# Recurrence, dense layer and expert layer in one program: chunks two to six issued as the source has them, attention units moved and stretched, expert rows fetched one slot earlier, scattered writes without mutual order

## The chip, the cores and the metric

One core of one Trainium2 chip runs the whole program in one launch. The metric is device time in microseconds (us), from the host-independent measurement of one execution; for the kernel before it is the median of three runs.

## What is computed

Three layers follow one another on 4 sequences of 768 tokens, 3072 tokens in all, 320 features.

```
for t in range(S):                       # gated recurrence, 8 heads of 40, per sequence
    m_new = max(f[t] + m, i[t])
    C = exp(f[t]+m-m_new) * C + exp(i[t]-m_new) * outer(v[t], k[t])
    n = exp(f[t]+m-m_new) * n + exp(i[t]-m_new) * k[t]
    y[t] = sigmoid(o[t]) * (C @ q[t]) / max(|n . q[t]|, 1)
x = y as 3072 x 320
h = x @ w_in;  x = (h * sigmoid(h)) @ w_out            # 320 -> 2048 -> 320
logits = x @ w_gate;  e = argmax(logits);  p = softmax(logits)[e]
out[token] = p * (relu(x @ w1[e]) @ w2[e])             # one of 8 experts, 320 -> 1024 -> 320
```

## The kernel before

**Tiles and stages.** A sequence is cut into 6 chunks of 128 tokens. A *unit* is one chunk of one sequence of the recurrence, all 8 heads, in closed form; there are 24, and the first four are done in a prologue. A unit's steps have names in the code: `load_unit` and `load_lam` (DMA in; `lam` is a 128x1024 table of gate sums, broadcast over partitions from `lam_d`, L202), `mask_lam` (POOL, L207), `prep_qk` (splits q and k in two halves of 16 bits; two DMA transposes, L230 and L234), `prep_exp` (ScalarE, L241), `at_S` (scores, matmuls L294, multiplied by `lam` on VectorE, L296), `at_I` and `at_C` (read and update of the state; its new halves are copied by two DMAs, L378 and L379), `at_PV` (matmuls L318, then a VectorE run that ends in y: L324 to L341), `at_X` (y is transposed on TensorE, L394, and read out by L397 on ScalarE and L400 on VectorE). The scores, state, PV and X results of all units share two PSUM buffers (`ps_at`, L66).

**The dense layer** takes chunk by chunk, 512 tokens of all four sequences at once, in 16 steps. A step is eight 128x512 matmuls (L959), a tanh on ScalarE (L975), a product on VectorE (L978), a 16-bit copy on ScalarE (L983) and its rest on VectorE (L986), and, two steps later (`LAG = 2`), twelve 128x328 matmuls (L1003 to L1005). Units of chunk c+1 are done beside the dense layer of chunk c. After a chunk, `rows(c)` picks the expert of each token, finds its place in a table `rows_x` in HBM and scatters the token there (indirect DMA of POOL, L929).

**The order.** Each step has two *slots* p. A table `plan` says at which slot a piece is traced; what a piece leaves to do is traced a slot later. The first slots of the units are in `base`; weights of experts 0 to 3 are loaded (`load_w`, L540 to L542, three DMAs of 704 KB together) and converted at slots of their own (L837). The traced order is only the source's: up to the end of chunk six the Tile scheduler sorts the instructions of each engine by its own cost model. From there, inside `tc.manual_schedule` (L1290), TensorE, ScalarE, VectorE and SyncE keep the order of the source. SyncE issues nearly all DMAs, one after another.

**The expert layer** is a line of 28 *places* of 128 rows each (three early ones, then three per expert, then four whose expert is a value read at run time). `get` (L1280) reads a row number from SBUF into a SyncE register (L1180), fetches 128 rows by a DMA transpose (L1183) into one of four buffers (Qs and Ks) and two numbers per row (L1188). `m_half` is 32 matmuls (L1203), twice per place; `m_l2` is 24 matmuls (L1222 to L1224) of the place before, a VectorE multiply (L1226), and an indirect DMA that scatters 128 finished rows into the output (L1234). Between them the weights of experts 4 to 7 and of the last four places are loaded into six staging buffers, three of them (`more`) free only from place 5 on, and converted on ScalarE and VectorE. To the scheduler all scatters write one tensor, the output.

```
        base = {n: PU * (n - B) - 2 for n in range(B, NC * B)}
        ...
            at(p + 4, at_PV, *cb)
            at(p + 4 + 3, at_X, *cb)
```

Of the kernel before, what the change touches and what calls it, by code (L numbers as in the profile page):

```python
# [8 lines left out]
F32 = mybir.dt.float32  # L9
# [24 lines left out]
def mlstm_moe_kernel(ctx, tc, q, k, v, ig, fg, og, w_in, w_out, w_gate, w1, w2, out):  # L34
    nc = tc.nc
# [13 lines left out]
    NG = 4  # L49
# [101 lines left out]
    vw_b, hb_b = carve(FIRST, (H, D1)), carve(FIRST, (H, D1))  # L151
    y_b = carve(FIRST, (384,))
    cl_b = carve(FIRST, (H, D1), F16)[0:D]
# [160 lines left out]
    def at_PV(c, b):  # L314
# [5 lines left out]
        def tail():  # L320
# [13 lines left out]
            nc.vector.reciprocal(out=den, in_=den)  # L334
            yt = y_b
            y = yt[:, 0:DM].rearrange("p (h d) -> p h d", d=D)
# [234 lines left out]
    with contextlib.nullcontext():  # L571
# [217 lines left out]
        def at(p, fn, *args):  # L789
            plan.setdefault(p, []).append((fn, args))  # L790


        PU = 2 * NF // B
        base = {n: PU * (n - B) - 2 for n in range(B, NC * B)}
        for i in range(B):
            base[B + i] = (1, 8, 15, 19)[i]
        for n in range(B, NC * B):
# [4 lines left out]
            if n > B:  # L802
                at(max(p - 9, base[n - 1] - 3), load_lam, *cb)
            at(p - 7, prep_qk, *cb)
# [7 lines left out]
            if cb[0] < NC - 1:  # L812
                at(p + 3, at_C, *cb)
            at(p + 4, at_PV, *cb)
            at(p + 4 + 3, at_X, *cb)

# [19 lines left out]
        for i in range(4 * NG):  # L836
            p = 2 * NF * 2 + 10 * i if i < 2 * NG else 2 * NF * (NC - 1) + 3 + 7 * (i - 2 * NG) // 2  # L837
            at(p, lambda i=i: w_go.append(load_w(i // NG, i % NG, i // NG)))
            at(p + (8 if i < 2 * NG else 7), lambda: w_go.pop(0)())
# [4 lines left out]
        def rows(c, b0=0, b1=B):  # L844
# [92 lines left out]

            return [experts, place, scale, weights] + [lambda b=b: halves(b) for b in range(nb)]

# [117 lines left out]
        passes = [(c, 0, B) for c in range(NC)]  # L1057
        p = 0
        for c, b0, b1 in passes:
            for f in range(NF):  # L1060
                tanh, prod, high, low = l1(c, f, b0, b1)
# [25 lines left out]
        while plan or late:  # L1087
            p = min([*plan, *late])
            run_late(p)
            run_at(p)  # L1090
        mp = ctx.enter_context(tc.tile_pool(name="mp", bufs=3, reuse_waits="tile"))
        rt = ctx.enter_context(tc.tile_pool(name="rt", bufs=1, reuse_waits="tile"))
# [119 lines left out]

        turn = [0]

        def m_l2(i, k, no):
# [16 lines left out]
            else:  # L1232
                nc.vector.tensor_tensor(out=sid, in0=no, in1=xm.pop(i)[:, 1:2], op=ALU.add)  # L1233
            nc.gpsimd.indirect_dma_start(  # L1234
                out=out[:, :], out_offset=bass.IndirectOffsetOnAxis(ap=sid, axis=0),
                in_=y, in_offset=None, bounds_check=NT - 1, oob_is_err=False,
            )


# [40 lines left out]
        def get(i):  # L1280
            if NE <= i < len(line):
                fetch(line[i][0], line[i][2])
# [4 lines left out]
        for _ in range(3):  # L1287
            load(None)
        ENG = mybir.EngineType
        with tc.manual_schedule(engines={ENG.PE, ENG.Activation, ENG.DVE, ENG.SP}):  # L1290

            for cf in todo:
                l2(*cf)
            for i in range(2):
                rowt.append(th_v[i][:, 0:RW])
                nc.gpsimd.memset(rowt[-1][:, 352:384], 0.0)
            experts, place, scale, weights, *halves = rows(NC - 1)
            half = lambda i, r: m_half(line[i][0], line[i][1], r)
# [19 lines left out]
            second(0)  # L1318
            for i in range(NE, NE + 2):
                get(i)  # L1320
            for i in range(2, len(line)):
                if i > 2:
                    get(i + 2)
                t = half(i, 0)
# [10 lines left out]
                split()  # L1335
                if i == 5:
                    for x in more:
                        load(x)
                second(i - 1)
# [42 lines left out]
```

## Time and profile before

| | us |
|---|---|
| median of 3 runs (lowest, highest) | 773.44 (769.42, 777.27) |
| the profiled execution, device time | 771.19 |
| its span, first to last instruction | 769.5 |
| TensorE busy in the span | 674.0 (88%) |
| VectorE, ScalarE busy | 516.6, 374.5 |
| mean granted TensorE clock | 0.947 |

Times in the profile count from the first instruction. Chunk one of the dense layer begins at 46.9, chunks two to six at 159.6, 247.2, 326.4, 406 and 478.7; the expert places begin at 538.1, and TensorE's last matmul ends at 757.0. The granted clock is a share of 2.4 GHz; it has two levels, 1.0 and 0.5. "DMA share" is the time that packets took, as a share of the core's 16 DMA engines.

### The profile page before, as it was taken

To read this page: it belongs to the slowest core of one execution; us is meant where nothing else is said; L and a number is where in the kernel's file an instruction comes from. 1 tells how busy PE (TensorE), PEld (TensorE's weight loads), DVE (VectorE), ACT (ScalarE), POOL (GpSimd) and SP (SyncE) were. 2 spreads that over 40 slices of the span, in tenths; PEclk is the share of its full clock that TensorE was granted. 3 is DMA by queue.
4 is the path that set the end of the run, shared out by engine and by line. 5 is a ranking of instruction groups with operands and counts; after the bars stand their busy time and mean duration, and the time that the engine had idled before them with its cause. 6 is when DMAs were issued, how large, how long until landed. Compare 5 with 4: busy or idle time off the path is not lost.

```text
span 769.5 us, 15581 instructions
## 1 busy us (share of the span) xinstructions
PE 674.0 (88%) x5840; PEld 477.4 (62%) x5840; DVE 516.6 (67%) x1262; ACT 374.5 (49%) x816; POOL 102.5 (13%) x134
## 2 busy tenths in 40 slices
PE   4858999998787898988999898999898799988993
PEld 3725766765444465655665564556787677777882
DVE  6777788895888776667577775844686275656631
ACT  4654466676656455555477434543334244334420
POOL 3110101102101121002100200110211021111211
PEclk9867799999999999998999999999999799999997
DMA  8767999987889855454533315420258999999800
GB/s 157 147 140 205 212 169 213 233 167 167 181 176 180 140 126 101 93 93 93 114 77 73 97 39 149 125 63 2 61 128 183 153 195 187 178 181 166 152 15 14
DMA packets 242827, 102.81 MB, mean 134 GB/s; under 512 B 181141, under 2 KB 236632, under 8 KB 242744
## 3 DMA queue, kind: packets, MB, share of 16 engines
q1 hardware_dynamic: 239380, 92.98, 61.7%
q0 software_dynamic: 2880, 8.68, 3.3%
q8 instruction: 48, 0.79, 0.5%
q14 instruction: 35, 0.29, 0.1%
q10 hardware_dynamic: 484, 0.08, 0.1%
HBM read 71.64 MB, written 11.59 MB: 108 GB/s over the span
## 4 chain that ended last, share of the span: by engine, by line
PE 42%; DMA 22%; DVE 15%; ACT 8%; issue 6%; SPq 3%; POOL 2%; POOLq 0%; ACTq 0%; DVEq 0%
PE ps_h L959 11%; PE ps_m L1203 9%; DMA w_all<-lam_d 5%; DMA Qs<-rows_x 4%; DMA out_dram<-ym,sid 3%; PE ps_y L1000 3%; DMA e<-in_moe_w_dram 3%; PE ps_pv L318 3%; ACT w_all L241 2%; DMA w_all<-Qs 2%; PE ps_y L1003 2%; DVE w_all L978 2%; PE ps_y L1004 2%; PE ps_y L1005 2%; POOL w_all L207 2%
## 5 line engine op out<-in xcount | busy, mean ns | idle before, releaser
L959 PE MATMUL ps_h<-w_all 128*128 128x512 f16 x768 | 197.1, 398 | 5.5 <-ACT w_all L466 3.5
L959 PEld LDWEIGHTS <-w_all 128*128 128x128 f16 x768 | 75.2, 102 | 84.0 <-issue 15.2
L1203 PEld LDWEIGHTS <-w_all 128*128 128x128 f16 x1792 | 105.8, 100 | 25.2 <-DMA Qs<-rows_x 13.0
L1003 PE MATMUL ps_y<-w_all 128*128 128x328 f16 x332 | 101.0, 304 | 2.0 <-ACT w_all L1011 2.0
L1004 PE MATMUL ps_y<-w_all 128*128 128x328 f16 x332 | 100.7, 303 | 0.0
L1005 PE MATMUL ps_y<-w_all 128*128 128x328 f16 x332 | 100.6, 303 | 0.0
L1208 ACT ACTIVATE hh<-ps_m 128x512 f16<-128x512 f32 x56 | 33.3, 595 | 132.6 <-PE ps_m L1203 120.0
L986 DVE SCALAR_TENSOR_TENSOR w_all<-w_all 128x512 f16<-128x512 f32 x83 | 57.2, 689 | 48.5 <-ACT w_all L983 48.0
L983 ACT ACTIVATE w_all<-w_all 128x512 f16<-128x512 f32 x83 | 51.8, 624 | 49.2 <-DVE w_all L978 48.6
L1209 DVE SCALAR_TENSOR_TENSOR hl<-ps_m,hh 128x512 f16<-128x512 f32 x56 | 38.5, 689 | 54.1 <-ACT hh L1208 53.4
L978 DVE SCALAR_TENSOR_TENSOR w_all<-w_all,ps_h 128x512 f32<-128x512 f32 x83 | 56.6, 682 | 24.9 <-ACT w_all L975 24.6
L241 ACT ACTIVATE w_all<-w_all,bias_t 128x128 f32<-128x128 f32 x160 | 52.9, 392 | 40.2 <-POOL w_all L207 40.1
L1224 PE MATMUL ps_m<-w_all,hl 128*128 128x320 f16 x224 | 67.0, 299 | 0.0
L1222 PE MATMUL ps_m<-w_all,hh 128*128 128x320 f16 x224 | 67.0, 299 | 0.0
L1223 PE MATMUL ps_m<-w_all,hh 128*128 128x320 f16 x224 | 67.0, 299 | 0.0
L1203 PE MATMUL ps_m<-Qs,w_all 128*128 128x128 f16 x896 | 54.8, 224 | 13.5 <-DMA Qs<-rows_x 11.7
L975 ACT ACTIVATE w_all<-ps_h 128x512 f32<-128x512 f32 x83 | 48.6, 586 | 34.3 <-PE ps_h L959 33.3
L1203 PE MATMUL ps_m<-Ks,w_all 128*128 128x128 f16 x896 | 54.1, 222 | 7.4 <-DMA Ks<-rows_x 6.7
L207 POOL TENSOR_SCALAR_AFFINE_SELECT w_all<-w_all 128x1024 f32<-128x1024 f32 x20 | 24.4, 1219 | 233.7 <-DMA w_all<-lam_d 146.2
L1234 POOL DMA_INDIRECT out_dram<-ym,sid x28 | 32.0, 1141 | 176.3 <-DVE sid L1233 128.5
L318 PEld LDWEIGHTS ps_pv<-w_all 128*128 128x128 f32 x384 | 50.2, 205 | 6.5 <-issue 2.1
L318 PE MATMUL ps_pv<-w_all 128*128 128x41 f32 x384 | 49.9, 291 | 3.1 <-issue 1.5
(213 smaller groups left out, 1152.6 us busy)
## 6 DMA issues: line engine op xcount, KB each, us to landing
e<-in_moe_w_dram SPq DMA_DIRECT2D x34, 320.0 KB
w_all<-lam_d SPq DMA_DIRECT2D x20, 512.0 KB
e<-in_moe_w_dram SPq DMA_DIRECT2D x34, 256.0 KB
w_all<-in_moe_w_out_dram SPq DMA_DIRECT2D x16, 320.0 KB
w_all<-in_moe_w_dram SPq DMA_DIRECT2D x14, 320.0 KB
e<-in_moe_w_dram SPq DMA_DIRECT2D x34, 128.0 KB
wi<-in_moe_w_in_dram SPq DMA_DIRECT2D x8, 512.0 KB
w_all<-in_k_dram SPq DMA_DIRECT2D x24, 160.0 KB
```

The source lines that it names most:

```text
L241: nc.scalar.activation(out=lt[:, h, :], in_=lt[:, h, :], func=AF.Exp, bias=bias_t[:, c, b * H + h:b * H + h + 1])
L318: nc.tensor.matmul(pv[:, h, :], u["lam"][:, h, :], u["v"][:, h, :], start=True, stop=True)
L959: nc.tensor.matmul(ps, a, x, start=(i == 0), stop=(i == len(terms) - 1))
L978: nc.vector.scalar_tensor_tensor(out=th, in0=th, scalar=1.0, in1=ps, op0=ALU.add, op1=ALU.mult)
L986: nc.vector.scalar_tensor_tensor(out=gl, in0=th, scalar=SG, in1=gh, op0=ALU.mult, op1=ALU.subtract)
L1003: nc.tensor.matmul(ps, gh[:, ts], woh[:, f, :], start=(f == 0), stop=False)
L1004: nc.tensor.matmul(ps, gh[:, ts], wol[:, f, :], start=False, stop=False)
L1005: nc.tensor.matmul(ps, gl[:, ts], woh[:, f, :], start=False, stop=(f == NF - 1))
L1203: nc.tensor.matmul(ps[:, jj, :], w1c[k][:, a, f * 128:f * 128 + 128], x[:, m, :], start=(n == 0), stop=(n == len(terms) - 1),)
L1222: nc.tensor.matmul(ps, hh[:, f, :], w[:, 0, :], start=(f == 0), stop=False)
L1223: nc.tensor.matmul(ps, hh[:, f, :], w[:, 1, :], start=False, stop=False)
L1224: nc.tensor.matmul(ps, hl[:, f, :], w[:, 0, :], start=False, stop=(f == NF2 - 1))
```

## The change

Four things change, and what is computed stays the same.

1. `tc.manual_schedule` is entered at chunk two (`c == 1`) and left after the last planned piece, so that TensorE, ScalarE, VectorE and SyncE keep the source's order there too. POOL stays with the scheduler, as does chunk one.
2. The units' slots. From chunk four's on, a unit begins 7 slots earlier relative to the dense steps (`- 9` instead of `- 2`); chunk three's four begin at 27, 34, 41, 48 (were 30, 38, 46, 54). `at_PV` comes a slot later, `at_X` eight or twelve slots after the unit's first (was seven), `load_lam` no earlier than six slots after the start of the unit two before. y gets a second buffer. Loads of experts 2 and 3 begin 10 slots earlier. `rows` does its `place` after `scale` and `weights`.
3. Places are fetched three ahead instead of two, and the three staging buffers `more` are taken one at places 5, 6 and 7 each, not all at 5.
4. The scatters into the output are declared independent of each other.

```diff
-    y_b = carve(FIRST, (384,))
+    y_b = turns([carve(FIRST, (384,)), const.tile([128, 384], F32, name="y2")])
...
-        base = {n: PU * (n - B) - 2 for n in range(B, NC * B)}
-        for i in range(B):
-            base[B + i] = (1, 8, 15, 19)[i]
+        base = {n: PU * (n - B) - 9 for n in range(B, NC * B)}
+        for i, p in enumerate((1, 8, 15, 19, 27, 34, 41, 48)):
+            base[B + i] = p
...
-                at(max(p - 9, base[n - 1] - 3), load_lam, *cb)
+                at(max(p - 9, base[n - 1] - 3, base[n - 2] + 6 if n > B + 1 else 0), load_lam, *cb)
...
-            at(p + 4, at_PV, *cb)
-            at(p + 4 + 3, at_X, *cb)
+            at(p + 5, at_PV, *cb)
+            at(p + (8 if n < 2 * B else 12), at_X, *cb)
...
-            p = 2 * NF * 2 + 10 * i if i < 2 * NG else 2 * NF * (NC - 1) + 3 + 7 * (i - 2 * NG) // 2
+            p = 2 * NF * 2 + 10 * i if i < 2 * NG else 2 * NF * (NC - 1) - 7 + 7 * (i - 2 * NG) // 2
...
-            return [experts, place, scale, weights] + [lambda b=b: halves(b) for b in range(nb)]
+            return [experts, scale, weights, place] + [lambda b=b: halves(b) for b in range(nb)]
...
+        by_hand = {ENG.PE, ENG.Activation, ENG.DVE, ENG.SP}
+        in_order = ExitStack()
         for c, b0, b1 in passes:
+            if c == 1:
+                in_order.enter_context(tc.manual_schedule(engines=by_hand))
...
+        in_order.close()
...
+            for other in outs:
+                tc.declare_no_dep(put.ins, other.ins, reason="every token is written by one slot")
+            outs.append(put)
...
-            for i in range(NE, NE + 2):
-                get(i)
+            get(NE)
+            get(NE + 1)
             for i in range(2, len(line)):
-                if i > 2:
-                    get(i + 2)
+                get(i + 3)
...
-                if i == 5:
-                    for x in more:
-                        load(x)
+                if more and i > 4:
+                    load(more.pop(0))
```

How the instructions stand on SyncE for one unit of the middle chunks, before: the last lines are the unit's `lam` (L202), its v, its o and the next unit's k and q; L378 and L379 copy the new state of the unit that runs now.

```order
L234 DMA_TRANSPOSE w_all<-Qs_108 128x8x128
L378 DMA w_all<-w_all 40x328
L230 DMA_TRANSPOSE w_all<-Ks_110 128x8x128
L379 DMA w_all<-w_all 40x328
L202 DMA w_all<-lam_d 128x8x128
L182 DMA w_all<-in_v_dram 128x8x40
L189 DMA w_all<-in_o_gate_dram 128x8x40
L176 DMA w_all<-in_k_dram 128x8x40
L177 DMA w_all<-in_q_dram 128x8x40
```

And with the change, the same engine and stage:

```order
L378 DMA w_all<-w_all 40x328
L379 DMA w_all<-w_all 40x328
L202 DMA w_all<-lam_d 128x8x128
L230 DMA_TRANSPOSE w_all<-Ks_110 128x8x128
L234 DMA_TRANSPOSE w_all<-Qs_108 128x8x128
L176 DMA w_all<-in_k_dram 128x8x40
L177 DMA w_all<-in_q_dram 128x8x40
L182 DMA w_all<-in_v_dram 128x8x40
L189 DMA w_all<-in_o_gate_dram 128x8x40
```

Both times `lam` stands behind a pair of state copies. By the slots (copies at a unit's +5, `lam` at the unit's -9, units 8 apart) the pair now belongs to the unit two before, whose state is done two slots earlier; before, the scheduler had put `lam` behind the copies of the unit just before it.

On SyncE in the expert layer, before, around place 5: two of the staged loads (L540 to L542, into w_all) and then the fetch of place 8 into buffer Qs_107.

```order
L540 DMA w_all<-in_moe_w_dram 128x2x256
L541 DMA w_all<-in_moe_w_dram 128x1x256
L542 DMA w_all<-in_moe_w_dram 128x2x320
L540 DMA w_all<-in_moe_w_dram 128x2x256
L541 DMA w_all<-in_moe_w_dram 128x1x256
L542 DMA w_all<-in_moe_w_dram 128x2x320
L1180 TENSOR_LOAD kofi
L1180 ISA x2
L1183 ISA
L1183 DMA_TRANSPOSE Qs_107<-rows_x 128x6x128
L1188 ISA
L1188 DMA xms<-rows_x 128x2
```

And with the change (lines of the expert layer are numbered six higher there):

```order
L1186 TENSOR_LOAD kofi
L1186 ISA x2
L1189 ISA
L1189 DMA_TRANSPOSE Qs_107<-rows_x 128x6x128
L1194 ISA
L1194 DMA xms<-rows_x 128x2
L540 DMA e_6516<-in_moe_w_dram 128x2x256
L541 DMA e_6516<-in_moe_w_dram 128x1x256
L542 DMA e_6516<-in_moe_w_dram 128x2x320
L540 DMA w_all<-in_moe_w_dram 128x2x256
L541 DMA w_all<-in_moe_w_dram 128x1x256
L542 DMA w_all<-in_moe_w_dram 128x2x320
```

Twelve load DMAs stood between the fetches of places 7 and 8; now three do (those of place 4), and the loads that were staged ahead of it follow it, one at a time.

## Rows read from the trace of the kernel before

**Rows 1.** The page, part 4: shares of the chain that ended last.
```profile
PE 42%; DMA 22%; DVE 15%; ACT 8%; issue 6%; SPq 3%; POOL 2%; POOLq 0%; ACTq 0%; DVEq 0%
```
**Rows 2.** Busy time by stretch: us, then PE, PEld, DVE, ACT, POOL, clock, DMA.
```profile
46.90:159.60 112.70, 104.92 (x633) 71.60 (x633) 91.62 (x201) 67.11 (x190) 12.36 (x12) 0.90 0.89 196
159.60:247.20 87.60, 73.70 (x561) 45.50 (x558) 68.72 (x171) 52.07 (x110) 13.07 (x13) 0.96 0.90 176
159.60:478.70 319.10, 284.72 (x2131) 179.11 (x2129) 228.52 (x588) 176.48 (x384) 41.25 (x40) 0.97 0.59 121
478.70:538.10 59.40, 58.05 (x347) 33.63 (x347) 35.71 (x90) 26.65 (x49) 4.17 (x6) 1.00 0.24 66
538.10:757.00 218.90, 197.56 (x2469) 169.34 (x2467) 126.09 (x280) 78.49 (x127) 35.09 (x31) 0.97 0.76 141
601.40:712.60 111.20, 100.66 (x1233) 86.37 (x1233) 65.50 (x119) 44.44 (x70) 15.27 (x14) 0.96 1.02 180
```
**Rows 3.** Waits of TensorE, 159.6 to 478.7: who on whom, total us, times, longest.
```profile
PE ps_x L394 <- DVE w_all L340: 11.0, 5, 2.4
PE ps_s L294 <- DVE w_all L400: 9.6, 8, 2.8
PE ps_r L877 <- DVE cum L870: 3.3, 2, 1.7
```
**Rows 4.** The chain that ended last, 300 to 319 us: start, us, what.
```profile
300.51 4.07 DMA w_all<-lam_d
...
304.73 1.10 POOL w_all L207
...
307.44 1.46 ACT w_all L241 x5
...
318.65 3.99 DMA w_all<-lam_d
```
**Rows 5.** DMA issues in chunk two, 159.6 to 247.2.
```profile
e<-in_moe_w_dram SPq DMA_DIRECT2D x10, 320.0 KB
```
**Rows 6.** Waits of ScalarE, 159.6 to 478.7.
```profile
ACT w_all L241 <- POOL w_all L207: 38.4, 14, 5.4
...
ACT w_all L552 <- DMA e<-in_moe_w_dram: 17.2, 7, 4.5
```
**Rows 7.** Waits of TensorE in the expert layer, 538.1 to 757.
```profile
PE ps_m L1203 <- DMA Qs<-rows_x: 11.7, 4, 7.9
PE ps_m L1203 <- DMA Ks<-rows_x: 6.7, 3, 3.1
```
**Rows 8.** The chain that ended last, matmuls of single places.
```profile
601.45 6.06 PE ps_m L1203 x64
610.77 3.57 PE ps_m L1203 x64
617.61 3.57 PE ps_m L1203 x64
...
656.96 6.43 DMA Qs<-rows_x
...
680.40 5.39 PE ps_m L1203 x64
```
**Rows 9.** SyncE's issues in order of time, 640 to 657 us.
```profile
641.17 2.01 SPq L1183 DMA_TRANSPOSE Ks<-rows_x  x1
...
647.87 1.27 SPq L1183 DMA_TRANSPOSE Ks<-rows_x  x1
...
656.96 1.84 SPq L1183 DMA_TRANSPOSE Qs<-rows_x  x1
```
**Rows 10.** VectorE in order of time, the last row numbers (sid).
```profile
754.27 0.15 DVE L1233 TENSOR_TENSOR sid<-neg,xms 128x1 int32<-128x1 f32 x1
...
757.53 0.15 DVE L1233 TENSOR_TENSOR sid<-neg,xms 128x1 int32<-128x1 f32 x1
```
**Rows 11.** POOL in order of time, the last two scatters.
```profile
754.70 0.98 POOL L1234 DMA_INDIRECT out_dram<-ym,sid  x1 [5.86 <-DVE sid L1233]
759.70 0.98 POOL L1234 DMA_INDIRECT out_dram<-ym,sid  x1 [4.03 <-DMA out_dram<-ym,sid]
```

More of the change, by code (lines that the diff above doesn't have):

```diff
@@ L334, in tail @@
             nc.vector.reciprocal(out=den, in_=den)
-            yt = y_b
+            yt = next(y_b)
             y = yt[:, 0:DM].rearrange("p (h d) -> p h d", d=D)
@@ L1058, in mlstm_moe_kernel @@
         p = 0
+        ENG = mybir.EngineType
+        by_hand = {ENG.PE, ENG.Activation, ENG.DVE, ENG.SP}
+        in_order = ExitStack()
         for c, b0, b1 in passes:
+            if c == 1:
+                in_order.enter_context(tc.manual_schedule(engines=by_hand))
             for f in range(NF):
@@ L1211, in m_half @@
             )
-        turn = [0]
+        turn, outs = [0], []
         def m_l2(i, k, no):
@@ L1233, in m_l2 @@
                 nc.vector.tensor_tensor(out=sid, in0=no, in1=xm.pop(i)[:, 1:2], op=ALU.add)
-            nc.gpsimd.indirect_dma_start(
+            put = nc.gpsimd.indirect_dma_start(
                 out=out[:, :], out_offset=bass.IndirectOffsetOnAxis(ap=sid, axis=0),
@@ L1288, in mlstm_moe_kernel @@
             load(None)
-        ENG = mybir.EngineType
-        with tc.manual_schedule(engines={ENG.PE, ENG.Activation, ENG.DVE, ENG.SP}):
+        with tc.manual_schedule(engines=by_hand):
             for cf in todo:
@@ L1296, in mlstm_moe_kernel @@
                 nc.gpsimd.memset(rowt[-1][:, 352:384], 0.0)
-            experts, place, scale, weights, *halves = rows(NC - 1)
+            experts, scale, weights, place, *halves = rows(NC - 1)
             half = lambda i, r: m_half(line[i][0], line[i][1], r)
```

## The prediction

> **What bounds the kernel now.** I read the page's chain first: TensorE is 42% of what ended last, DMA 22%, VectorE 15% [rows 1]. So the end is set partly by matmuls and partly by waits between them, and the question is where these lie. The busy times by stretch answer it [rows 2]. In chunks two to six's first four, 159.6 to 478.7, TensorE is busy 284.7 of 319.1 us: 34.4 us idle. In chunk six, with no attention beside it, 58.05 of 59.40: 1.35 idle. In the expert layer 197.6 of 218.9: 21.3 idle. VectorE (228.5 of 319.1, 72%) and ScalarE (55%) have room in the mean.
>
> Then the waits of TensorE. In the four chunks it waits for y before X (11.0 us), for X's PSUM buffer before the next unit's scores (9.6), for the expert counts (3.3) [rows 3]. These look like small VectorE matters, but the chain shows why they come at all: `lam` of one unit is issued at 300.51, the next at 318.65 [rows 4], one unit every 18.1 us, and between the two stand its DMA (4.07), POOL's mask (1.10), the exponentials (1.46 for five), scores, y, state copies, and then the next `lam` on SyncE. That is one serial loop through five engines, and TensorE's own work per unit, 284.7/16 = 17.8, just fits into it. Every piece that the loop delays TensorE waits for. Chunk two is worse, 73.7 busy of 87.6 [rows 2], with the DMA engines 90% busy: the scheduler has pulled ten weight loads into it [rows 5], which the source puts into chunks three and later.
>
> In the expert layer TensorE waits almost only for rows: 11.7 and 6.7 us, 18.4 in seven waits [rows 7]. Undisturbed places start 6.84 apart (610.77, 617.61), but SyncE is slower: from 641.17 to 656.96 it issues two fetches and three loads without a pause, 15.8 us for two places, while TensorE would need 13.7 [rows 8, 9]. A fetch takes some 6.4 to land [rows 8], so it comes late whenever SyncE has fallen a place behind.
>
> **The change, part by part.** All against the profiled execution, 771.2 us (span 769.5; 2.2 below the median of 773.4, inside the runs' spread).
>
> *Order and slots, chunks two to five.* On SyncE `lam` now stands behind the state copies of the unit two before instead of one, so the loop spans two units, some 36 us, for a path of about 18: it no longer decides. X follows y by six slots instead of two, and y has two buffers; `place` comes after nine more small VectorE operations. So the waits of rows 3 lose their cause, and TensorE's own 17.8 per unit is what is left. What is late next? TensorE cannot run ahead of source order either, so VectorE bursts (a converted weight set beside a y run) will show. The two places that already run in source order tell how much: chunk six idles 1.35 of 59.4 (2.3%), and the expert layer 21.3 − 18.4 = 2.9 of 218.9 outside the row waits (1.3%). I take 2.3% of 285, 6.5 us. The granted clock was 0.97 over the stretch [rows 2]: 3%, 9.6 us, are missing from the full level, partly inside idle time; of this I credit 3. Sum: 34.4 + 3 − 6.5 = 31 us gained. From both sides: 9.6 more if all clock and no idle comes back (41), and half if the bursts cost 1 us per unit more (15).
>
> The DMAs that move: eight loads of 704 KB go from chunk two to slots ten apart in chunks three to five. DMA share over the four chunks is 0.59 [rows 2], so they find room; their conversion waits on ScalarE (17.2 us in all [rows 6]) get 8 slots, over 13 us, of lead.
>
> *Chunk one* stays with the scheduler, but gets the first slots of one more unit and loads for two, in a stretch where DMA is already 0.89 busy and the clock at 0.90 [rows 2]. Nearest rows: TensorE idles 7.8 of 112.7 there, so a gain of 3 is possible; a unit's work is 17.8, a third of it moved in is 6 lost here and regained later. I take 2 lost.
>
> *Chunk six.* It was nearly full: 1 of its 1.35 idle. Its weight loads start ten slots earlier, beside a DMA share of 0.24. 0 to 1.3.
>
> *Places fetched three ahead.* One place more of lead, 6.84 us [rows 8]. The longest wait, 7.9, followed the burst of twelve load DMAs between two fetches, which is gone; the other six are 3.1 or less [rows 7], under the new lead. All 18.4 would go, and with them 4.3 of slow matmuls after the gaps (6.06 and 5.39 instead of 3.57 [rows 8]). Against it, SyncE still needs 15.8 per pair. The fetches and loads go on over some 17 places, 8.5 pairs: at 2.1 lost per pair that is 18 us, and the lead covers 6.84. But 641.17's and 656.96's transposes took 2.01 and 1.84 where 647.87's took 1.27 [rows 9], in a stretch with the DMA engines at 1.02 [rows 2]; with 1.27 each the pair is 14.5, and 8.5 times 0.8 is the lead. I leave 4 us of waits: 18.4 + 4.3 − 4 = 18.7. From both sides: 7 and 23. The Trainium skill bears on this: Perfetto Trace Analysis, section "DMA Instruction — HWDGE (DVE, Sync)", says that such a row holds the wait for the descriptor generator's lock and none of the data's movement. By it the 2.01 is partly waiting, which fewer collisions would take away, and the sum is 719; without it the pair stays 15.8 and the time is the second rival's.
>
> *Independent scatters.* Only the last one waited for another's landing: POOL issued it at 759.70 after 4.03 idle [rows 11]. Its row numbers were done at 757.53 + 0.15; the scatter before went 0.28 after its own (754.42 to 754.70) [rows 10, 11]. So it can go at 757.96: 1.7 us. At worst 0, if the two then share the engines.
>
> Sum: 31 − 2 + 1 + 18.7 + 1.7 = 50.4; 771.2 − 50.4 = 720.8, forecast **721 us**. Its own range is 711 to 730.
>
> **The rivals.** *SyncE bounds the places.* 15.8 per pair holds, the lead is used up after three pairs, waits of 11 us remain; places gain 18.4 − 11 + 2 of clock = 9 instead of 18.7: 731. For it: no pause in 15.8 us [rows 9], DMA at 1.02. Against: the burst and the collisions are less.
>
> *Chunk two stays DMA-bound.* Units' loads, the table's first fill and transposes alone keep the engines full, and its 13.9 idle stays: some 12 of the 31 are lost, 733. Against: the ten loads leave.
>
> *Two PSUM buffers are the limit.* The 9.6 us before scores [rows 3] come from two shared buffers, not from the order, and stay: 730. The Trainium skill speaks for it: Perfetto Trace Analysis, "Optimization Strategy", says that the same gap repeating on the engine that should be full can mean too few buffers for the next tile, and no buffer of that kind is added here. The trace agrees that the gap repeats, eight times; that X waits for y just before (11.0) speaks for the order as its cause.
>
> *The order was not the limit.* The loop stays 18 to 20 us per unit by another path, DMA transposes or POOL, which the scheduler still orders; the four chunks gain nothing, 752.
>
> *Slower: ScalarE blocked in order.* A scheduled ScalarE put other work ahead of exponentials whose mask was late; it still waited 38.4 us for masks in 14 waits [rows 6]. In source order the next tanh stands behind them, and after it the product and, two steps on, TensorE. The path from `lam`'s issue to the fifth exponential is 300.51 to 308.9, 8.4 us [rows 4]. If half of it lies bare in every unit, a unit takes 17.8 + 4.2 = 22.0, the chunks 352 instead of 319.1, and with 19.4 gained elsewhere the time is 785. It decides from 3.8 bare per unit (21.6 per unit, 346: 1% slower). Against it: `lam` is issued nine slots, over 15 us, before the scores.
>
> **How the numbers follow.** Forecast 0.52; SyncE bound 0.17; chunk two 0.11; PSUM 0.08; order not the limit 0.05; slower 0.04; better than 708, where nearly all idle and clock comes back, 0.03. All but the last three lie in 706 to 745, with the forecast's own tails cut that is a little over 8 in 10. A run of this kernel tells about 1% from no change (7.7 us). Faster by more than that: all but the slower case and a part of the unknown, 0.92; within 1%, 0.04; slower 0.04.
>
> **What would show it.** Right: `lam` of successive units no longer in the chain, TensorE over 97% busy in chunks two to five, each of the first three some 72 us long; the ten loads out of chunk two; row waits under 5 us; the last scatter 0.3 after its row numbers. The single steps are wrong if chunk two still idles over 8 us, if waits on L400 stay near 9, or if waits for rows stay over 8. The whole is wrong if ScalarE's wait for masks grows and TensorE's idle time with it.

## The result and the profile after

| | before | after |
|---|---|---|
| median, us (lowest, highest; runs) | 771.43 (767.17, 777.27; 4) | 732.77 (729.6, 736.41; 4) |
| ratio, 95% interval | | 0.9495, 0.9414 to 0.9577 |
| profiled execution, span | 771.2, 769.5 | 736.4, 734.7 |

The forecast was 721 and its own range 711 to 730; 732.8 lies outside that and inside the 706 to 745 that holds the rivals too. Where the time went, in the two profiled executions:

| stretch | before | after | change | predicted |
|---|---|---|---|---|
| chunk one | 112.7 | 114.2 | +1.5 | +2 |
| chunks two to five | 319.1 | 290.2 | -28.9 | -31 |
| chunk six | 59.4 | 57.8 | -1.6 | -1 |
| expert places | 218.9 | 213.8 | -5.1 | -18.7 |
| after TensorE's last matmul | 12.5 | 11.5 | -1.0 | -1.7 |

The attention part went nearly as forecast; the expert places kept 13.6 us that were forecast to go. The chain of what ended last, after, which answers to [rows 1]:

```profile
PE 70%; DVE 13%; DMA 8%; ACT 3%; SPq 3%; issue 2%; POOL 0%; POOLq 0%; DVEq 0%; ACTq 0%
```

TensorE rises from 42% to 70% of the chain, DMA falls from 22% to 8%. Busy time by stretch, after, columns as in [rows 2] (chunk one, chunk two, chunks two to five, chunk six, the places, the loaded part of the places):

```profile
47.20:161.40 114.20, 104.26 (x616) 70.36 (x616) 90.09 (x198) 63.01 (x179) 11.90 (x13) 0.88 0.85 188
161.40:241.10 79.70, 75.74 (x628) 49.94 (x627) 63.47 (x159) 45.18 (x109) 13.25 (x14) 0.98 0.56 119
161.40:451.60 290.20, 280.59 (x2146) 181.52 (x2145) 233.97 (x577) 171.04 (x383) 39.63 (x40) 0.98 0.58 124
451.60:509.40 57.80, 57.80 (x350) 33.74 (x348) 44.75 (x106) 34.08 (x61) 4.16 (x6) 1.00 0.47 123
509.40:723.20 213.80, 198.40 (x2468) 170.29 (x2466) 126.55 (x280) 78.83 (x127) 35.11 (x31) 0.98 0.79 145
545.00:685.00 140.00, 127.81 (x1568) 109.87 (x1565) 82.84 (x149) 56.31 (x88) 21.19 (x18) 0.96 1.00 177
```

In chunks two to five TensorE's idle time falls from 34.4 to 9.6 us; in the places it falls only from 21.3 to 15.4. Waits of TensorE, after, first in chunks two to five, then in the places (they answer to [rows 3] and [rows 7]):

```profile
PE ps_it L304 <- DVE w_all L296: 2.9, 4, 1.5
PE ps_r L877 <- DVE w_all L367: 2.9, 2, 1.5
PE ps_r L877 <- DVE w_all L296: 2.7, 1, 2.7
PE ps_x L394 <- DVE w_all L308: 0.9, 1, 0.9
...
PE ps_m L1209 <- DMA Ks<-rows_x: 6.9, 3, 3.5
PE ps_m L1209 <- DMA Qs<-rows_x: 4.2, 2, 3.1
PE ps_m L1209 <- DVE hl L1215: 1.8, 3, 0.9
PE ps_m L1209 <- DVE w_all L560: 1.7, 1, 1.7
```

X no longer waits for y (11.0 before) nor the scores for X's readout on L400 (9.6). Of the row waits 11.1 of 18.4 us are left. One set of weights is left in chunk two where ten stood [rows 5]:

```profile
e<-in_moe_w_dram SPq DMA_DIRECT2D x1, 320.0 KB
```

And ScalarE's waits for masks, 38.4 us in [rows 6], over chunk one to the last place, after:

```profile
ACT w_all L241 <- POOL w_all L207: 2.3, 3, 1.4
```

What keeps the places waiting stands in SyncE's issues, after: start, us, what. L542 is the third load of a set, L1189 the fetch.

```profile
500.63 0.48 SPq L542 DMA_DIRECT2D e<-in_moe_w_dram  x1
501.22 0.40 SPq L540 DMA_DIRECT2D e<-in_moe_w_dram  x1
501.66 0.54 SPq L541 DMA_DIRECT2D e<-in_moe_w_dram  x1
502.25 1.98 SPq L542 DMA_DIRECT2D e<-in_moe_w_dram  x1
...
569.70 1.95 SPq L542 DMA_DIRECT2D e<-in_moe_w_dram  x1
...
572.78 2.86 SPq L542 DMA_DIRECT2D e<-in_moe_w_dram  x1
...
577.22 3.12 SPq L542 DMA_DIRECT2D w_all<-in_moe_w_dram  x1
581.31 1.90 SPq L1189 DMA_TRANSPOSE Ks<-rows_x  x1
...
587.89 1.26 SPq L1189 DMA_TRANSPOSE Qs<-rows_x  x1
```

The same load is issued in 0.48 us when it comes first and in 1.95 to 3.12 in the other rows, which have one or more sets issued in the few us ahead of them. From 568.60 to 580.34 nine loads keep SyncE 11.7 us without a pause, and the fetch that comes next (581.31) is that of place 11, which TensorE could have begun at 585.1 and begins at 587.70. Not only its issue is late. Its rows are there 6.3 us after the issue begins, where the last packets of the four fetches from 525.57 to 534.39, with few or no loads beside them, are done after 2.5 to 2.9.

### The profile page after: what moved, and what is told of

Same layout as the page of the kernel before. It is cut to its first block, busy times and chain, and to the rows that moved or that the text cites. A ratio compares the mean times of both kernels' runs of the same rounds, so it can differ in the third digit from the quotient of the medians.

```text
span 734.7 us, 15579 instructions
## 1 busy us (share of the span) xinstructions
PE 671.2 (91%) x5840; PEld 480.0 (65%) x5840; DVE 529.7 (72%) x1262; ACT 372.7 (51%) x816; POOL 100.6 (14%) x134
## 4 chain that ended last, share of the span: by engine, by line
PE 70%; DVE 13%; DMA 8%; ACT 3%; SPq 3%; issue 2%; POOL 0%; POOLq 0%; DVEq 0%; ACTq 0%
PE ps_h L959 19%; PE ps_m L1209 12%; PE ps_y L1003 5%; PE ps_y L1005 5%; PE ps_y L1004 5%; PE ps_pv L318 5%; DMA Ks<-rows_x 3%; PE ps_y L1000 3%; PE ps_m L1228 3%; PE ps_m L1230 3%; PE ps_m L1229 3%; DMA Qs<-rows_x 2%; PE ps_wg L517 1%; DMA wi<-in_moe_w_in_dram 1%; DMA w_all<-lam_d 1%
## 5 line engine op out<-in xcount | busy, mean ns | idle before, releaser
L959 PE MATMUL ps_h<-w_all 128*128 128x512 f16 x768 | 193.1, 392 | 8.2 <-ACT w_all L466 5.1
L959 PEld LDWEIGHTS <-w_all 128*128 128x128 f16 x768 | 73.5, 100 | 85.1 <-issue 10.6
L983 ACT ACTIVATE w_all<-w_all 128x512 f16<-128x512 f32 x83 | 51.6, 622 | 30.7 <-DVE w_all L978 28.9
L1209 PE MATMUL ps_m<-Ks,w_all 128*128 128x128 f16 x896 | 55.9, 226 | 8.9 <-DMA Ks<-rows_x 6.9
L241 ACT ACTIVATE w_all<-w_all,bias_t 128x128 f32<-128x128 f32 x160 | 50.2, 391 | 2.4 <-POOL w_all L207 2.3
L207 POOL TENSOR_SCALAR_AFFINE_SELECT w_all<-w_all 128x1024 f32<-128x1024 f32 x20 | 22.8, 1142 | 183.1 <-DMA w_all<-lam_d 130.0
```

The lines of the kernel that those rows point to most:

```text
L959: nc.tensor.matmul(ps, a, x, start=(i == 0), stop=(i == len(terms) - 1))
L983: nc.scalar.activation(out=gh, in_=th, func=AF.Copy, scale=SG)
L1209: nc.tensor.matmul(ps[:, jj, :], w1c[k][:, a, f * 128:f * 128 + 128], x[:, m, :], start=(n == 0), stop=(n == len(terms) - 1),)
```

## The experiments

e1 to e4 undo the four parts of the change one at a time (y's second buffer and the new order inside `rows` stay in all of them), e5 to e10 ask why rows are still late, c1 and c2 put together what helped. "Places" is from the first matmul of the expert layer to the last; times by stretch are of each one's profiled execution. The medians and 95% intervals (ratio to the kernel before, measured beside them):

| run | what | median | interval | chunks 2-5 | places | row waits |
|---|---|---|---|---|---|---|
| | the change | 732.77 | 0.941-0.958 | 290.2 | 213.8 | 11.1 |
| e1 | fetch two ahead | 736.95 | 0.948-0.959 | 284.8 | 218.0 | 15.6 |
| e2 | scheduler's order | 755.67 | 0.972-0.983 | 310.5 | 212.9 | 13.2 |
| e3 | old slots | 727.74 | 0.936-0.946 | 279.6 | 219.7 | 13.8 |
| e4 | scatters wait | 731.56 | 0.931-0.951 | 284.2 | 214.3 | 9.6 |
| e5 | loads by ScalarE | 750.28 | 0.964-0.972 | 285.2 | 226.7 | 0 |
| e6 | 64-row part once | 711.69 | 0.916-0.927 | 285.1 | 195.5 | 0 |
| e7 | rows not transposed | 723.70 | 0.926-0.943 | 283.4 | 204.9 | 8.3 |
| e8 | sets earlier | 739.49 | 0.954-0.958 | 284.4 | 217.4 | 14.9 |
| e9 | e6, fetch two ahead | 713.22 | 0.917-0.929 | 284.8 | 195.0 | 0 |
| e10 | 64-row part, half columns | 713.24 | 0.910-0.924 | 285.2 | 195.0 | 0 |
| c1 | e6 with old slots | 708.73 | 0.912-0.922 | 280.5 | 195.0 | 0 |
| c2 | e6, old starts alone | 711.58 | 0.908-0.922 | 275.5 | 195.1 | 0 |

One thing helps to read it: e1 and e4 to e10 issue the attention part just as the change does, and need 283 to 285 us for chunks two to five; the change's profiled execution lost 5 us more in chunk three (76.1 instead of 71), and its device time is 3.6 over its median.

**e1: the fetch part undone.**

```diff
-                get(i + 3)
+                if i > 2:
+                    get(i + 2)
...
-                if more and i > 4:
-                    load(more.pop(0))
+                if i == 5:
+                    for x in more:
+                        load(x)
```

> The changed kernel with the fetch part alone undone: rows two places ahead, the three further staging buffers all loaded at place 5. Theory A (the prediction's term was right in kind, its cover was lost to the DMA engines or to SyncE): in the changed kernel the places took 213.8 us with 11.1 us of waits for rows, in the kernel before 218.9 with 18.4, so undoing it gives back some 5 us: median near 738, places 217 to 220, row waits 16 to 20. Rival B (the fetch part was worth its 18.7 us, and the order part or the later start cost the places some 13): median near 751, places 227 or more. Rival C (the fetch part is worth nothing, the lower waits came from somewhere else): median 731 to 735.

Waits of TensorE in its places:

```profile
PE ps_m L1209 <- DMA Qs<-rows_x: 9.3, 3, 6.0
PE ps_m L1209 <- DMA Ks<-rows_x: 6.3, 3, 3.2
```

The places take 4.2 us more, the median rises by 4.2. So the part was worth about 4 us, as theory A said; the intervals of the two ratios overlap, so this is likely and not certain. The rest of the 18.7 did not come from it.

**e2: the source's order undone.**

```diff
-            if c == 1:
-                in_order.enter_context(tc.manual_schedule(engines=by_hand))
```

> The changed kernel with the source's order taken out of chunks two to six, its new slot table kept: the scheduler sorts TensorE, ScalarE, VectorE and SyncE there again. Theory (the order is what frees the loop of one lam per unit; the slots alone are only a wish to the scheduler): the 28.9 us gained in chunks two to five are mostly lost again, median 750 to 765, weight loads back in chunk two, TensorE idle 20 us or more in chunks two to five. Rival (the slots did it, the scheduler follows them well enough): median 733 to 740, idle under 13.

Chunk two, and chunks two to five:

```profile
162.20:251.60 89.40, 76.72 (x580) 48.82 (x578) 65.56 (x170) 51.09 (x112) 13.51 (x12) 0.94 0.93 158
162.20:472.70 310.50, 281.31 (x2099) 179.41 (x2097) 231.92 (x594) 176.89 (x384) 41.74 (x39) 0.97 0.66 129
```

29 us idle again, a DMA share of 0.93 in chunk two, seven sets of weights there, and ScalarE waits 27.1 us for masks. With the new slots, the order is worth 22.9 us; the slots alone do not bring it.

**e3: the old slots in the source's order.**

```diff
-        base = {n: PU * (n - B) - 9 for n in range(B, NC * B)}
+        base = {n: PU * (n - B) - 2 for n in range(B, NC * B)}
...
-            at(p + 5, at_PV, *cb)
-            at(p + (8 if n < 2 * B else 12), at_X, *cb)
+            at(p + 4, at_PV, *cb)
+            at(p + 4 + 3, at_X, *cb)
```

(with the first units' slots, `lam`'s rule and the loads of experts 2 and 3 as before.)

> The changed kernel with the source's order kept but the old slot table: units start seven slots later, lam may be loaded three slots before the unit before begins, X stands seven slots after the unit's first instead of eight or twelve, weights of experts 2 and 3 are loaded ten slots later. Theory (order and slots need each other: in strict order an X that stands two slots behind PV blocks TensorE for y in each of 16 units): waits of X for y and of scores for X's readout come back at 1 to 2.5 us per unit, 16 to 40 us, median 750 to 770. Rival (the order alone did it, the slots are trimming): median 733 to 738.

The theory fell. Chunk one, chunk two, and chunks two to five; then the longest of TensorE's waits in the last:

```profile
47.00:156.70 109.70, 100.02 (x633) 67.01 (x633) 88.81 (x197) 64.47 (x181) 13.60 (x12) 0.95 0.85 192
156.70:226.30 69.60, 68.71 (x561) 44.77 (x558) 57.85 (x144) 41.90 (x95) 11.57 (x12) 1.00 0.61 114
156.70:436.30 279.60, 272.03 (x2131) 176.50 (x2128) 233.85 (x577) 171.30 (x380) 40.20 (x40) 1.00 0.64 131
```

```profile
PE ps_s L294 <- DVE w_all L400: 4.9, 5, 2.9
```

X two slots behind PV costs 4.9 us in all, not one to two and a half per unit. `lam` stands behind the state copies here as in the change (copies at 238.64 and 239.53, `lam` at 240.34, one unit every 16 us), so the source's order gives the loop its two units without the new slots. The new table adds chunk two's ten us (79.7 against 69.6) and gets 4.4 back in chunk five and 1.0 in chunk six: it moves attention forward. Chunk two's cost comes back in every other run with the new table in the source's order (78.0 to 79.8) and in none with the old starts (68.2 to 69.7); chunk one's time differs from run to run (109.7 here, 112.3 in c1, 110 to 118 with the new table). Against that, the places take 5.9 us more here than in the change, with a wait of 2.6 us for the expert counts (0.5 in the change). In the medians the new table is 5 us worse; the two intervals overlap, so the sign is likely and not certain.

**e4: the scatters ordered again** (the three lines with `declare_no_dep` taken out).

> The changed kernel with the scatters again ordered behind each other. Theory (only the last scatter waits for the landing of the one before): the end after TensorE's last matmul goes from 11.5 to 12.5 to 13.2 us, the median rises by 1.0 to 1.7, nothing else changes. Rival 1 (scatters also wait inside the line, and hold y buffers and then VectorE): more than 3 us. Rival 2 (nothing: the two last scatters share the DMA engines and end together anyway): 0.

The last scatter on POOL in e4, and after it the one of the change:

```profile
719.77 0.98 POOL L1240 DMA_INDIRECT out_dram<-ym,sid  x1 [3.29 <-DMA out_dram<-ym,sid]
```

```profile
724.11 0.98 POOL L1240 DMA_INDIRECT out_dram<-ym,sid  x1 [2.28 <-DVE sid L1239]
```

Its row numbers are done at 718.34 + 0.15 in e4 and 723.69 + 0.15 in the change: 1.28 of waiting against 0.27. But both programs end 11.5 us after TensorE's last matmul (729.3 - 717.8, 734.7 - 723.2): the scatter that starts 1.1 us earlier lasts 1.1 longer (10.6 against 9.5 to the end). Rival 2: worth nothing that shows.

**e5: the expert layer's loads issued by ScalarE** (`nc.sync` becomes `nc.scalar` in the loads that the places issue).

> The changed kernel with the three weight loads of each set in the expert layer (L540 to L542, L545 to L547) issued by ScalarE instead of SyncE, so that SyncE issues only the fetches there. In the changed kernel the places take 213.8 us, with 11.1 us of waits for rows. Theory A (SyncE's time for issuing bounds the places): a fetch alone keeps SyncE some 2.6 us per place of 6.8, the row waits fall under 3, the places take 200 to 204, the median is 719 to 724. Theory B (the DMA engines are full, and SyncE's issues are long because they wait for room): row waits stay over 7, or the same time shows as ScalarE's issues of 2 to 3 us and waits of TensorE for PSUM, the places take 210 to 218, the median is 730 to 738.

The longest of TensorE's waits in its places, and two of ScalarE's:

```profile
PE ps_m L1211 <- DVE hl L1217: 26.6, 20, 4.2
```

```profile
ACT hh L1216 <- issue: 22.3, 6, 5.5
ACT hh L1216 <- DMA e<-in_moe_w_dram: 10.6, 3, 6.2
```

No row is late any more. That fits SyncE as late with the fetches, but does not show it alone: the places take 12.9 us more, so each row also has more time. But ScalarE's own work now stands behind the loads in its order: ahead of L1216 (the readout of the first matmuls) lie 10.6 us of waits for staged weights and 22.3 us in which it waits for nothing that the profile shows and its issues stand ahead, and TensorE waits 26.6 us for what follows from them. The Trainium skill (Perfetto Trace Analysis, "DMA Optimizations") says that balancing DMAs over the engines that can issue them may help where descriptor generation is the bottleneck. Here it ends the waits it should end, and the kernel is 17.5 us slower, because ScalarE keeps the source's order and is on the path (in the profiled executions the places are 12.9 us longer and chunk six 6.1).

**e6: the 64-row part once.** The 64 rows of L541 (L546 for the last four places) went to both halves of the partitions; now they go to one, and the remainder is taken from there. This part is the middle one of a set's three issues; the issue that stretches, L542, follows it.

```diff
-            nc.sync.dma_start(out=t[:, 2, :], in_=bcast0(w1[e, 256:320, cs], 2))
+            nc.sync.dma_start(out=t[0:64, 2, :], in_=w1[e, 256:320, cs])
...
-                    out=o1[64:128, 2, :], in0=t[64:128, 2, :], scalar=SW1, in1=o1[64:128, 2, :],
+                    out=o1[64:128, 2, :], in0=t[0:64, 2, :], scalar=SW1, in1=o1[0:64, 2, :],
```

> The changed kernel with the third part of each set (64 rows of w1) loaded once to 64 partitions instead of twice to 128: 576 KB in 512 packets instead of 704 KB in 640, as many issues; VectorE takes the remainder from the lower partitions, ScalarE's conversion is two instructions instead of one. Theory A (SyncE's issues): the row waits stay within 2 us of 11.1, the median within 3 of 732.8. Theory B (DMA engines full): 18% of the loads' packets leave the stretch where the engines' share is 1.01, the issues of the third load fall from 2 to 3 us to under 1.5, row waits 3 to 7, the places take 204 to 209, the median is 722 to 728.

More than theory B hoped for. Three third issues of e6, the first of them with a set just ahead of it as at 502.25 above, and a fetch; then the busy time of its loaded stretch:

```profile
493.96 0.59 SPq L542 DMA_DIRECT2D e<-in_moe_w_dram  x1
...
559.87 0.59 SPq L542 DMA_DIRECT2D e<-in_moe_w_dram  x1
...
561.53 0.59 SPq L542 DMA_DIRECT2D w_all<-in_moe_w_dram  x1
562.91 1.26 SPq L1190 DMA_TRANSPOSE Ks<-rows_x  x1
```

```profile
540.00:665.00 125.00, 125.00 (x1620) 108.51 (x1618) 83.93 (x153) 60.14 (x119) 21.80 (x19) 1.00 0.84 199
```

1.98 to 3.12 became 0.59, the fetch 1.26; TensorE does not pause in 125 us. The places lose 18.3 us (213.8 to 195.5), about what the prediction had hoped to get from the lead.

**e7: rows by a plain DMA** (`dma_start` for `dma_start_transpose`).

> The changed kernel with the rows of places 3 to 27 fetched by a plain DMA instead of a DMA transpose: it leaves the transposition out, so the matmuls multiply rows that are not turned; bytes and number of fetches are the same. In the changed kernel's 573 to 685 the 9984 packets of 256 B of 13 transposes took 53 of the 112 us of the 16 engines, 85 ns each in the mean, where such packets took 21 ns in 509 to 530, beside no loads. Theory B1 (transposes in the middle of loads hold the engines): with 128 packets of 1536 B per fetch the engines' share falls under 0.85, the third load's issue to under 1 us, row waits under 2, the places take 199 to 203, the median is 718 to 723. Theory B2 (the loads' bytes fill the engines, whatever the form of the fetch): the share stays over 0.95 and the row waits over 6. Theory A (SyncE): a plain issue takes some 0.4 instead of 1.27 to 2, so the row waits halve, the third load's issue stays at 2 us.

```profile
565.36 1.11 SPq L540 DMA_DIRECT2D e<-in_moe_w_dram  x1
566.51 0.59 SPq L541 DMA_DIRECT2D e<-in_moe_w_dram  x1
567.14 2.98 SPq L542 DMA_DIRECT2D e<-in_moe_w_dram  x1
...
571.69 3.14 SPq L542 DMA_DIRECT2D w_all<-in_moe_w_dram  x1
```

```profile
540.00:680.00 140.00, 131.29 (x1677) 112.15 (x1676) 90.05 (x163) 59.67 (x94) 22.34 (x19) 1.00 0.66 192
```

B1 and B2 both fall: the engines' share is 0.66, and the third issue still takes 2.98 and 3.14, and TensorE still waits 8.3 us for rows. The fetch itself got cheaper for SyncE (0.32 in the mean of 19 issues in the loaded stretch, against 1.71 of 16 in the change), the third issue dearer (1.83 against 1.56 in the mean), and the row waits fell by 2.8 us only. The places still lose 8.9 us: in the loaded stretch the granted clock is 1.00, against 0.96 in the change. Of the three, theory A comes closest.

**e8: three sets converted earlier.**

```diff
-            for cf in todo:
-                l2(*cf)
+            l2(*todo[0])
+            split()
+            l2(*todo[1])
+            low_and_load()
...
             t()
+            split()
+            low_and_load()
             second(0)
+            split()
```

> The changed kernel with the first three staged sets of the expert layer converted some three places earlier (one beside the last matmuls of chunk six, one beside place 1, one beside place 2), so that three loads move from the stretch with a DMA share of 1 into 509 to 536, where it is 0.21. Theory B (DMA engines full): the full stretch ends two places earlier, row waits 5 to 8 instead of 11.1, the median is 726 to 731. Theory A (SyncE): the same by as many issues, 726 to 731; it does not tell A from B but whether a lead at the start is kept. Rival (the lead is used up within a few places, as with the third place of fetching): row waits 9 to 13, the median 731 to 735. Against it stands a delay of place 3's rows by the 1.9 us that VectorE converts before it has done the row numbers: up to 2 us.

A miss: 6.7 us slower. The lead does not last (row waits 14.9), chunk six grows by 2.7, and the DMA share is back at 0.89 from 530 on. This fits the rival, a head start that is used up, but as the run also puts VectorE work ahead of place 3's row numbers, it does not show it alone.

**e9 and e10: is it the lead, and is it the number of packets?** e9 is e6 with e1's edit. e10:

```diff
-            nc.sync.dma_start(out=t[:, 2, :], in_=bcast0(w1[e, 256:320, cs], 2))
+            nc.sync.dma_start(out=t[:, 2, 0:nf], in_=bcast0(w1[e, 256:320, g * GF:g * GF + nf], 2))
```

> The run e6_once (third part of each set loaded once: 711.69 us, places 195.4, no waits for rows) with rows fetched two places ahead again. Theory (with lighter loads SyncE is no longer late, so a third place of lead has little left to cover): row waits 1 to 5 us, median 712 to 717, so the fetch part alone was never worth the 18.7 that was predicted; what cures the waits is the lighter load. Rival (the lead of three places was needed as well, and only the full rings hid it): row waits 10 or more, median 722 or more.

> The changed kernel with the third part of each set of experts 4 to 7 and of the last four places loaded to 128 partitions as before, but only half of its columns: it leaves out the other half of these columns, whose weights are replaced by the first half's. As many packets as in the changed kernel (640 per set), 128 of them of 512 B instead of 1024 B, 640 KB instead of 704; e6_once had 512 packets and 576 KB. Theory P (the number of packets in the rings decides): the third load's issue stays at 1.1 to 2.1 us in the mean, row waits 8 to 12, the median is 729 to 735. Theory Q (the bytes decide): about half of what e6_once gained, row waits 3 to 6, the median 718 to 726.

With lighter loads a lead of two places does as well as three (195.0 against 195.5, no row late): the third place by itself was worth nothing there. And e10 does as well with as many packets as the change, 9% fewer bytes: theory P falls, and Q was too modest. Its loaded stretch:

```profile
540.00:670.00 130.00, 130.00 (x1678) 112.68 (x1676) 88.06 (x161) 62.26 (x122) 22.37 (x19) 1.00 0.95 196
```

The engines are 0.95 busy and TensorE never waits; in e7 they were 0.66 busy and it did. So it is not the engines' mean share that decides. What sorts these runs is the time that SyncE spends issuing DMAs, summed over its 110 to 122 rows in the loaded stretch: 103.5 of 141 us in the kernel before, 102.4 of 140 in the change, 97.3 of 140 in e7 (all three with row waits), 83.8 of 130 in e10, 76.8 of 125 in e9, 70.7 of 125 in e6 (without). The third issue took 1.56 us there in the change, 1.83 in e7, 0.63 in e10, 0.50 in e9 and 0.47 in e6, each the mean of 26 to 28.

Why it stretches, the packets of the kept traces show in part. Four stretches, columns as in [rows 2]: the end of two sets that the change issues from 499.61 on with little beside them; the time of its issue at 577.22; the end of the same two sets in e10; and most of them in e6.

```profile
507.10:509.50 2.40, 2.40 (x21) 1.70 (x20) 0.93 (x3) 1.18 (x3) 0.12 (x1) 1.00 0.15 52
578.70:580.70 2.00, 2.00 (x40) 2.00 (x38) 1.94 (x6) 0.60 (x1) 0.96 (x1) 1.00 0.14 46
501.50:502.50 1.00, 1.00 (x9) 0.71 (x8) 0.44 (x1) 0.53 (x1) 0.00 (x0) 1.00 0.14 44
494.00:497.00 3.00, 3.00 (x20) 1.80 (x19) 1.09 (x2) 1.15 (x2) 0.00 (x0) 1.00 0.89 280
```

In the first three the DMA share is 0.14 or 0.15, as much as two of the 16 engines, and nearly all that moves are packets of one size: 1 KB in the change, 512 B in e10. Of the loads only e10's halved 64-row part has packets of 512 B. So it is this part, 128 packets from rows that are read twice, that runs some two packets at a time while most engines have nothing to do. In e6, where the rows are read once, no such end follows: its two sets take 5.7 us from first to last packet, against 10.8 in the change and 8.4 in e10. An estimate from the second row (90 packets in 2 us): the part takes 2.8 us per set, 74 of the 140 us for the change's 26 sets, and about half of that in e10. It fits e7 too, where one to three packets are under way in 20% of the loaded stretch, and none in 0.3%. That the long issues and the late rows wait for this part is read from times that coincide: no run spread the same bytes over more engines. And e6 and e10 both convert each set with one more ScalarE instruction, which no run has alone.

**c1 and c2: put together.** c1 is e6's edit and e3's; c2 takes only the units' old first slots from e3.

> The two runs that beat the changed kernel together: the source's order with the old slot table (e3_old_slots, 727.74) and the third part of each set loaded once (e6_once, 21.1 under the changed kernel). If they add up: median 702 to 711, chunk one 108 to 110, chunks two to five 278 to 281, the places 195 to 200, no waits for rows. Rival (the late loads of experts 2 and 3 in the old table still delay the start of the expert layer, with a wait for the expert counts of 2.6 us and slow matmuls after it): places 199 to 203.

> As c1_old_slots_once, but only the first slots of the units are the old ones: PV and X one and several slots later, lam's rule and the ten slots earlier loads of experts 2 and 3 are those of the changed kernel. Theory (what costs in the new table is the earlier start, which moves attention into chunks one and two; X far behind y is a gain): the 4.9 us in which scores wait for X's readout in e3_old_slots go, the expert layer starts without the wait for counts, the median is 3 to 8 under c1_old_slots_once. Rival (X late in the table is what costs): chunk two 75 or more, the median 3 or more above it.

In c2, X of a chunk's last unit stands two slots behind the first step of the pass that reads it, so that the first two of sixteen steps work on older features there; its time is to be read with that. c1 is the best of all, 708.73: 24 us under the change, and 8.3% under the kernel before. The two gains nearly add up (706.7 would be the sum); against e6 alone the intervals overlap. Loads that are lighter also end the wait at the start of the expert layer that e3 had. Theory and rival for c2 are both not borne out: it is not under c1, and its chunk two takes 68.2.

## Why the prediction was right or wrong

*Chunks two to five, -31.* Right in size (28.9 in the profiled execution, 34 to 36 in the other kernels with the same code there), half right in its reason. Most signs came as named: `lam` fell from 5% to 1% of the chain, nine of ten sets left chunk two, the waits on L400 went, TensorE is 96.7% busy (over 97 was forecast), and chunk four takes 71 us (chunk three 76.1 here, and 71 in the other kernels with the same code). The step that failed in it is "order and slots" as one cause: e3 shows that the order does it without the new slots, and that these give part of it back in chunk two, which takes 79.7 and not 72. The 6.5 us of remaining idle time were 9.6 here and 7.6 in e3; they were taken from chunk six as one of "the two places that already run in source order", but before the change the scheduler still sorted that chunk. The upper bound of 41 is too low by its own words: all clock and no idle gives 34.4 + 9.6 = 44.

*Chunk one, +2, and chunk six, -1:* +1.5 and -1.6. For chunk one that is luck: its reason was a third of a unit moved in, but TensorE's busy time there did not grow (104.26 us, 104.92 before), and the chunk takes 110 to 118 us in the runs with the same code there.

*Places fetched three ahead, -18.7:* the term that failed; 5.1 came, 4.2 of them from the edit (e1). The step is "with 1.27 each the pair is 14.5, and 8.5 times 0.8 is the lead; I leave 4 us of waits". It let the fetch's issue become short again by itself, and took the loads' issues for fixed. The runs show the reverse: the third load's issue is what stretches, to 2 or 3 us, in the change as before, the fetches are issued late and land late, and 11.1 us of waits remain. The rows were also misread. The fetch at 656.96 stands outside the pair that begins at 641.17, so the pair with short fetches is 15.0 and not 14.5, 11.5 us lost in 8.5 pairs, which the lead of 6.84 does not cover. And the issues in these 15.8 us add up to 9.5, so "without a pause" is not what their rows show. The 11.1 us are over the 8 that the prediction names as a sign of a wrong step. The outcome is nearest to the rival *SyncE bounds the places*: its 11 us of waits left are the 11.1 measured, and its 731 is closer to 732.8 than the forecast, though it gave the places a gain of 9 us and not 5.1. e6 and e10 (no late row once the 64-row part is lighter and SyncE's issues are short) bear it out; e5 and e8 fit it. Its reason, SyncE's own pace, is only half of it: SyncE is slow where the 64-row parts ahead of it still run.

The Trainium skill's section that the prediction weighed there (Perfetto Trace Analysis, "DMA Instruction — HWDGE (DVE, Sync)") has an issue's row hold a wait and none of the data's movement. The rows fit that, and for the load more than for the fetch: the same load took 0.48 and 3.12 us, the fetch 1.26 and 1.90. By its rule the prediction had expected the fetch's wait to shrink with fewer collisions; it shrank where the loads became lighter (1.71 us in the mean in the change, 1.24 in e6).

*Independent scatter, -1.7:* the mechanism was right (0.27 after its row numbers, 0.3 forecast), the gain was the lower bound, 0: in e4 the end is as long, and the 1.0 us in the table above is not this part's.

*Other rivals.* Chunk two is not DMA-bound any more (share 0.56, was 0.90). The two PSUM buffers were not the limit: they are as before, and the waits on L400 went. So the rule of the Trainium skill that the prediction put behind that rival (Perfetto Trace Analysis, "Optimization Strategy"), that a gap that repeats can mean too few buffers, is not borne out for these two; whether y's second buffer had a part, no run shows. ScalarE is not blocked: 2.3 us of waits for masks.

The sum: 732.8 against 721 is 11.8 us over, and the places' term alone is 13.6 over.

What stays open is the last step: that a third load's issue, and the fetch behind it, wait for the two or so engines on which the 64-row part runs. It is neither the engines' mean share (0.66 in e7, 0.95 in e10) nor the number of packets alone (e10 has the change's). The part's time fits: e10's issue at 497.22 still took 1.64 us, while packets of 512 B ran from 496.45 on, and e6's at 493.96 took 0.59. But no run varied the spread alone.

## What to carry to other kernels

A lead pays once; where the queue that issues the fetches is slower than the work that uses them, look for what makes its issues long, and cut that, before lengthening the lead. Read the duration of each DMA's issue row on the issuing engine: when one form of load takes 0.5 us alone and 2 to 3 behind others, look at what the loads ahead do. A mean share of the DMA engines can hide it: look for stretches in which only one load is left, and at how many engines it keeps busy. And when a change sets both an order and a table of slots, try each alone: here the order was the gain, and the table by the medians was not.

## What the runs showed of the hardware

- An issue's duration on SyncE is not a property of the instruction: 0.48 us and 3.12 us for the same 320 KB load, 1.26 and 1.90 for the same transposing fetch.
- Taking 128 of a set's 704 KB away (e6), or 64 of them with as many packets (e10), ended all waits for rows, 11.1 us, and with them the slow matmuls behind the gaps (granted clock 0.96 to 1.00 in the loaded stretch): 18 us for 9 to 18% of the sets' bytes.
- A load of 64 rows that are read twice, to both halves of the partitions, ran at a DMA share of 0.14, as much as two of the 16 engines, and 44 to 46 GB/s, with next to nothing else moving (e10, 501.5 to 502.5, where the packets' size tells it apart, and the change, 578.7 to 580.7); the sets that read the rows once ran at 0.89 and 280 GB/s (e6, 494 to 497).
- A DMA share near 1 is not yet a bound (e10: 0.95, no wait), and 0.66 is no proof of room (e7).
